# Subtracting attention thresholds on GpSimd for eight pairs of heads, in place of a second score pass for two of them

## The chip, the cores and the metric

The kernel runs on one core of a Trainium2 chip. The metric is device time in microseconds for one execution; lower is better. The core has engines that each work through their own list of instructions in order and wait for one another by semaphores: TensorE (PE, matmuls), VectorE (DVE), ScalarE (ACT), GpSimd (POOL), and SyncE (SP), which here only issues transfers.

## The reference

Attention with a threshold, for 8 batches of 8 heads with 576 positions and 64 channels, followed by a feed-forward block on the 4608 tokens.

```python
scores = scale * np.matmul(q, k.transpose(0, 1, 3, 2))
thresh = np.max(scores, axis=-1, keepdims=True) - tau
scores = np.where(scores >= thresh, scores, -1000000000.0)
scores = scores - np.max(scores, axis=-1, keepdims=True)
attn = np.exp(scores)
attn = attn / (np.sum(attn, axis=-1, keepdims=True) + 1e-09)
attn_out = np.matmul(attn, v)
# (B,H,S,D) -> (B*S, H*D) is x, 4608 x 512
h = x @ w_in                                   # 512 x 2048
g = h * (1.0 / (1.0 + np.exp(-1.702 * h)))
out = g @ w_out                                # 2048 x 512
```

q, k and v are float32; the two weight matrices arrive as float64 and are turned into float32 on the chip.

## The kernel before

**Pairs.** Two heads of a batch make a pair, so there are 32 pairs, four to a batch, numbered from 0 here as in the code. Scores are kept transposed: keys on partitions, queries along the free dimension. A pair has nine steps of 64 keys per head (two heads and two halves of the queries fill 128 partitions and 576 columns). Two steps make a tile of 128x1152, so a pair has four such tiles, 0 to 3, and tile 4, which has one step and 576 columns.

**What is done for a pair `n`.** `load_qk` and `load_v` issue the transfers (SP). `prep` transposes q and k (DVE, L498). `scores` computes a step on PE (L514), `keep` copies it from PSUM to SBUF (ACT, L531), `in_groups` takes maxima of a tile (DVE, L537), `over_tiles` and `over_halves` finish the maximum and take the gap off it. The threshold of each query must then stand on all partitions that hold its column. There are three ways to that:

- `spread_max`: one transpose on DVE (L618).
- by DMA (pairs in BY_DMA): `turn_rows` on DVE, `row_out` to DRAM (L627) and `row_in` back with the row repeated (L636), both issued by SP.
- by a second score pass (pairs in TWICE): `row_blocks` on DVE (L585, L587) places the thresholds for a matmul; `again` computes each step of scores a second time on PE and adds minus the threshold by a second group of matmuls (L604); `mask_one` reads that from PSUM on ACT (L612), one step at a time.

In the first two ways `sub` (L642) subtracts the thresholds from a tile in SBUF, and `mask` (L648) makes everything below zero hugely negative. In all three, `exps` (L652) takes exponentials of a tile on ACT. `values` multiplies by v on PE (L663) and `sums_by_pe` by ones (L663, into `den`); in later pairs the sums are `in_groups` with add on DVE, and `turn_sums`, `sums_out` and `sums_in` send their reciprocals through DRAM. `place_x` (DVE, L765) divides and writes the result into x, transposed.

**Feed-forward.** x is cut into 18 blocks of 256 tokens. The first two (`first_blocks`) go through `mm1_0` (L820), `tanh`, `gelu_0` (L826) and `mm2` (L802); the first needs all four pairs of batch 0. Later blocks use `mm1` (L780) and seven products (`product`, L971) in place of eight, whose sums of halves are made by POOL (`s_sums`, L937 to L939, and `s_last`); the last four blocks use seven products for the first matmul too (`product1`, L885; `w_sum` L859, `x_sum` L868).

**Weights.** There are 32 pieces, 16 of w_in and then 16 of w_out. For each, POOL issues two DMAs (`load_w`, L449 and L450), DVE takes the exponent (L460), masks and combines the mantissa (L474, L478), ACT turns the exponent to a power of two (L468), and DVE multiplies (`cv_end`, L486). Pieces pass through a few slots; a load waits until its slot has been freed by an earlier `cv_end`. The first six loads are held back behind q and k of pairs 2 and 3 by `hold`.

**Order.** Nothing is scheduled by hand and nothing by the framework: each step is a `task` with an engine, a cost in microseconds, a rank and its predecessors, and `run_in_order` plays them in a list schedule while the program is being built. Whenever an engine is free in that play, it takes the ready task of lowest rank whose buffers are free, and the instructions are emitted in that order. A step's rank is the pair's number plus a bias from one of four tables: EARLY for pairs 0 to 3, SECOND for 4 to 7, LATER for the rest, CV for the weights. W_RANK gives the base ranks of the weight pieces. Transfers are tasks of two servers of their own, DMS for those that SP issues and DMW for the weights. The order that results is fixed in the program; on the chip each engine follows it, whatever the real durations are.

The ways in which pairs differ are set by a few constants:

```python
JOINT = 7
TWICE = (2, 3)
BY_POOL = {}
SUMS_BY_PE = (0, 1, 2, 3, 4)
BY_DMA = (0, 1, *range(4, NP))
SUMS_BY_DMA = range(5, NP)
SHARED = 0.2 if BY_POOL else 0.0
```

JOINT is the first pair whose scores are interleaved on PE with the values of the pair two before it. BY_POOL maps a pair to the tiles whose `sub` runs on POOL; it is empty, so every `sub` runs on DVE. SHARED is added to the planner's cost of two weight steps on DVE.

Of the kernel before, what the change touches and what calls it, by code (L numbers as in the profile page):

```python
# [30 lines left out]
def kernel(  # L31
# [97 lines left out]
    for x in ("raw0", "raw1", "qkT0", "qkT1", "mb"):  # L129
# [3 lines left out]


    EARLY = {
        "again": -7.56,
        "exps": -11.91,
        "in_groups": 11.71,
        "keep": 5.71,
        "load_qk": 5.18,  # L140
        "load_v": 30.97,
        "mask": 4.9,
        "mask_one": 3.1,
        "one_group": -15.86,
        "one_row": 7.15,
        "over_halves": -2.83,
        "over_tiles": 6.14,
        "place_x": -3.25,
        "prep": 2.3,
        "row_blocks": 1.94,  # L150
        "row_in": 22.91,
        "row_out": -2.33,
        "scores_run": 18.47,
        "spread_max": -1.73,
        "spread_sums": 1.81,
        "sub": 11.02,
        "sums_by_pe": -0.88,
        "sums_in": -30.06,
        "sums_out": 1.15,
        "turn_rows": 7.89,  # L160
        "turn_sums": 3.77,
        "values": 12.67,
        "w_sum": -3.43,
        "x_sum": -40.7,
    }
    SECOND = {
        "again": 1.9,
        "exps": -5.59,
        "in_groups": 24.66,
        "keep": 31.08,  # L170
        "load_qk": 4.38,
        "load_v": 10.96,
        "mask": 1.77,
        "mask_one": -3.71,
        "one_group": 2.55,
        "one_row": -9.14,
        "over_halves": -14.0,
        "over_tiles": 20.14,
        "place_x": -19.87,
        "prep": 13.95,  # L180
        "row_blocks": -7.77,
        "row_in": -19.84,
        "row_out": -10.94,
        "scores_run": -8.9,
        "spread_max": -3.11,
        "spread_sums": 11.27,
        "sub": 23.58,
        "sums_by_pe": 28.33,
        "sums_in": 6.64,
        "sums_out": 8.13,  # L190
        "turn_rows": -23.75,
        "turn_sums": -20.53,
        "values": -5.6,
        "w_sum": 2.52,
        "x_sum": -6.03,
    }
    LATER = {
        "again": 0.33,
        "exps": -3.93,
        "in_groups": 13.94,  # L200
        "keep": -8.05,
        "load_qk": -10.23,
        "load_v": -5.75,
        "mask": 20.67,
        "mask_one": 13.2,
        "one_group": 4.78,
        "one_row": -18.27,
        "over_halves": -1.32,
        "over_tiles": -0.36,
        "place_x": 19.41,  # L210
        "prep": -1.19,
        "row_blocks": -5.02,
        "row_in": 1.23,
        "row_out": 9.63,
        "scores_run": -23.96,
        "spread_max": -9.44,
        "spread_sums": 7.45,
        "sub": 5.73,
        "sums_by_pe": -10.99,
        "sums_in": -0.62,  # L220
        "sums_out": -1.68,
        "turn_rows": 3.05,
        "turn_sums": 5.98,
        "values": -17.83,
        "w_sum": -2.8,
        "x_sum": 11.74,
    }
    CV = {
        "cv_end": -4.16,
        "cv_ex": -2.85,  # L230
        "cv_frac": -20.95,
        "cv_power": -9.52,
        "load_w": -10.23,
    }

    LAG = {"PE": 0.26, "DVE": 0.18, "ACT": 0.22, "POOL": 0.18, "SP": 0.1}
# [4 lines left out]
    def task(engine, cost, rank, f, *a, after=(), take=(), give=(), lag=None):  # L241
        if lag is None:
            lag = LAG[engine]
        if 0 <= rank < LAST:
            biases = EARLY if a[0] < NPAIR else SECOND if a[0] < 2 * NPAIR else LATER
            rank += CV[f.__name__] if f.__name__ in CV else biases.get(f.__name__, 0.0)
        tasks.append((engine, cost, rank, f, a, [x for x in after if x is not None],
                      take, give, lag))
        return len(tasks) - 1
# [71 lines left out]

    rebias = const.tile([P, 1], FP32, name="rebias")
    JOINT = 7
    TWICE = (2, 3)
    BY_POOL = {}

# [45 lines left out]
    def own(n, *pools):  # L374
        return tuple(x + "_apart" for x in pools) if n in APART else pools
# [134 lines left out]
    def scores(n, j):  # L510
        ps = psA.tile([P, 2, 512], FP32, name="ps", tag="ps")
        for h in range(2):
            for c in range(2):
# [4 lines left out]
                )  # L518
        if j == NK - 1 and n not in TWICE:
            del mats[n, 0], mats[n, 1]  # L520
# [32 lines left out]
    def over_halves(n):  # L553
        r = stats[n, ALU.max]
        o = work.tile([P, QB], FP32, name="fold", tag="fold", bufs=1)
        for x in (1, 3) if n in BY_DMA else range(4):
            nc.vector.tensor_scalar(
                out=o[ts(x ^ 1, 32)], in0=r[ts(x, 32)], scalar1=gap[ts(x, 32)], scalar2=None,
                op0=ALU.subtract,
            )  # L560
        if n in TWICE:
            for x, y in ((0, 0), (1, 2), (2, 1), (3, 3)):
# [4 lines left out]
            return  # L567
        if n in BY_DMA:
            for x in (0, 2):
# [69 lines left out]
    def sub(n, t):  # L639
        s = sT[n, t].rearrange("p u h s -> p u (h s)")  # L640
        engine = nc.gpsimd if t in BY_POOL.get(n, ()) else nc.vector
        engine.tensor_tensor(  # L642
# [361 lines left out]
    NP = B * NPAIR  # L1004
# [38 lines left out]


    SUMS_BY_PE = (0, 1, 2, 3, 4)
    BY_DMA = (0, 1, *range(4, NP))
    SUMS_BY_DMA = range(5, NP)
    LEAD = 6
    WHOLE = 6

    SHARED = 0.2 if BY_POOL else 0.0
    FFU = 1.727
    T_RANK = FIRST

    W_RANK = (8.59, 39.29, 35.34, 31.13, 0.54, 8.21)
    ready_w, w_loads, w64 = [], [], 0
    for i in range(len(pieces)):
        y = 0 if i < NDC else 2 if i < n_in else 4
        n = NDC if i < NDC else n_in - NDC if i < n_in else n_in
        first = (0, 0, NDC, 0, n_in)[y]  # L1060
        rank = W_RANK[y] + (W_RANK[y + 1] - W_RANK[y]) * (i - first) / n
        if not wide:
# [205 lines left out]
    for n in range(NP):  # L1268
# [64 lines left out]
        else:  # L1333
            for js in [range(x, x + 3) for x in range(0, NK, 3)] if n >= WHOLE else [[x] for x in range(NK)]:
# [3 lines left out]
                    take=("psA",) * len(js) + new,  # L1338
                    give=own(n, "qkT0", "qkT1") if js[-1] == NK - 1 and n not in TWICE else (),
                )  # L1340
# [3 lines left out]
        a = task("DVE", 0.35, r, over_tiles, n, ALU.max, after=mx)  # L1344
        quick = n in BY_DMA or n in TWICE
        a = task(
            "DVE", 1.05 if not quick else 1.3 if n in TWICE else 0.8, r, over_halves, n,
            after=[a, tau_done], take=("row",) if quick else (),
        )
        if n in TWICE:  # L1350
            m = task("DVE", 0.6, r, row_blocks, n, after=[a], take=own(n, "mb"), give=("row",))
        elif n in BY_DMA:
            a = task("DVE", 0.21, r, turn_rows, n, after=[a])
# [7 lines left out]
        for t in range(NKT + 1):  # L1361
            tail = t == NKT
            if n in TWICE:
# [7 lines left out]
                continue  # L1371
            pool = t in BY_POOL.get(n, ())
            a = task(
                "POOL" if pool else "DVE", (1.45 if pool else 0.67) if tail else 2.7 if pool else 1.35,
                r, sub, n, t, after=[y for y, x in subs if tail or x in (None, pool)],
# [89 lines left out]
```

## Time and profile before

| | |
|---|---|
| times of three runs | 1336.89, 1333.9, 1336.76 us; median 1336.76 |
| the profiled execution | 1336.89 us, span 1335.1 us |
| PE busy | 1278.8 us, 96% |
| DVE busy | 990.5 us, 74% |
| ACT busy | 647.7 us, 49% |
| POOL busy | 248.1 us, 19% |
| chain that ended last | PE 67%, DVE 12%, DMA 8%, ACT 7% |
| L514, scores | 2304 matmuls, 172.4 us |
| L604, the second score pass | 288 matmuls, 24.1 us |
| L642, `sub` on DVE | 149 instructions, mean 1306 ns |
| L652, `exps` on ACT | 160 instructions, mean 1249 ns |

Busy time is how long an engine had an instruction in work; the difference of span and PE's busy time, 56.3 us, is what TensorE stood idle. Consecutive matmuls overlap, so that their own durations add up to more than the busy time. The shares are means over a start, in which loading, conversion of weights and the first pairs are all under way, and a long steady part. In rows of the timeline the first two numbers are the start from the beginning of the span and the length in microseconds, and brackets at the end tell how long the engine stood idle before it and what it waited for.

### The profile page before, as it was taken

The numbers are of one execution on the slowest core, as the hardware profiler recorded it, in microseconds if no ns is written. First come the engines' busy times: TensorE is split into PE (matmuls) and PEld (weight loads), VectorE is DVE, ScalarE is ACT, GpSimd is POOL, SyncE is SP. The second block draws the span as 40 slices with busy tenths as digits, with TensorE's granted clock in tenths as the row PEclk, the third lists the DMA queues.
The fourth block names the chain that finished last, engine by engine and source line by source line (L and its number), as shares of the span: only waits on it lengthen the run. The fifth ranks groups of instructions, "written<-read, shape, count | busy, mean of one in ns | idle before, by whom it ended". The sixth has DMA issues, their size and how long they took to land.

```text
span 1335.1 us, 23381 instructions
## 1 busy us (share of the span) xinstructions
PE 1278.8 (96%) x9416; PEld 988.3 (74%) x9416; DVE 990.5 (74%) x1600; ACT 647.7 (49%) x838; POOL 248.1 (19%) x301
## 2 busy tenths in 40 slices
PE   5599799899999999999999999999999999999998
PEld 2456585457777777778878777777777878888887
DVE  6798799888887788778877777778877863652642
ACT  4786465767454555555455445455555540210210
POOL 1121111003112120212130201112121216120120
PEclk8799899999999999999999999999999999999999
DMA  8579686547232222222323232222222120000000
GB/s 152 212 161 271 226 250 124 106 91 124 63 70 55 57 44 59 55 53 55 70 54 70 46 79 55 62 47 50 55 55 53 37 61 2 16 1 24 8 1 32
DMA packets 259634, 103.53 MB, mean 78 GB/s; under 512 B 233926, under 2 KB 244934, under 8 KB 259526
## 3 DMA queue, kind: packets, MB, share of 16 engines
q1 hardware_dynamic: 245798, 64.00, 22.8%
q0 software_dynamic: 11360, 37.74, 9.4%
q8 instruction: 74, 1.21, 0.4%
q10 hardware_dynamic: 2368, 0.30, 0.2%
q14 instruction: 34, 0.28, 0.1%
HBM read 88.10 MB, written 9.70 MB: 73 GB/s over the span
## 4 chain that ended last, share of the span: by engine, by line
PE 67%; DVE 12%; DMA 8%; ACT 7%; SPq 3%; issue 2%; DVEq 0%; POOL 0%; ACTq 0%
PE ops L971 22%; PE hps L780 16%; PE pv L663 8%; PE ps L514 8%; PE ps L885 4%; PE ps L971 4%; DVE part L537 3%; ACT arena L652 3%; PE ops L885 3%; DMA arena<-row 3%; DVE arena L642 3%; ACT arena L648 2%; DMA arena<-in_k_dram 2%; DMA arena<-in_q_dram 1%; PE hps L820 1%
## 5 line engine op out<-in xcount | busy, mean ns | idle before, releaser
L537 DVE TRANSPOSE_TENSOR_REDUCE part<-arena 128x36 f32<-128x1152 f32 (+1 forms) x295 | 359.6, 1239 | 63.6 <-ACT arena L531 54.0
L780 PE MATMUL hps<-xT,w_in 128*128 128x256 f32 x1536 | 339.8, 381 | 5.9 <-DVE arena L792 5.6
L780 PEld LDWEIGHTS hps<-xT,w_in 128*128 128x128 f32 x1536 | 289.8, 190 | 54.8 <-DVE arena L792 10.7
L648 ACT ACTIVATE arena<-arena 128x1152 f32<-128x1152 f32 (+1 forms) x150 | 158.5, 1057 | 164.7 <-DVE arena L642 164.7
L531 ACT COPY arena<-ps 128x576 f32<-128x576 f32 x288 | 170.3, 645 | 140.4 <-PE ps L514 140.4
L642 DVE TENSOR_TENSOR arena<-arena 128x1152 f32<-128x1152 f32 (+1 forms) x149 | 188.4, 1306 | 37.7 <-DMA arena<-row 37.7
L971 PE MATMUL ops<-w_out,arena 128*128 128x256 f32 x896 | 203.3, 381 | 1.6 <-DVE arena L792 1.3
L652 ACT ACTIVATE arena<-arena,shift,scl 128x1152 f32<-128x1152 f32 (+1 forms) x160 | 199.9, 1249 | 4.1
L514 PE MATMUL ps<-arena 64*64 64x288 f32 x2304 | 172.4, 416 | 23.1 <-DVE neg L1030 8.3
L971 PEld LDWEIGHTS ops<-w_out,arena 128*128 128x128 f32 x896 | 168.9, 190 | 30.3 <-DVE arena L792 4.2
L937 POOL TENSOR_TENSOR arena<-arena 128x256 f32<-128x256 f32 x56 | 49.1, 877 | 651.6 <-DVE arena L792 540.6
L663 PE MATMUL pv<-arena 64*64 64x288 f32 x2176 | 160.0, 409 | 0.0
L971 PE MATMUL ops<-arena 128*128 128x256 f32 x672 | 150.6, 380 | 0.0
L514 PEld LDWEIGHTS ps<-arena 64*64 64x64 f32 x2304 | 84.8, 136 | 86.7 <-ACT arena L531 24.6
L971 PEld LDWEIGHTS ops<-arena 128*128 128x128 f32 x672 | 127.2, 190 | 19.3 <-issue 2.2
L789 ACT ACTIVATE th<-hps 128x512 f32<-128x512 f32 x112 | 65.9, 589 | 142.8 <-PE hps L780 127.9
L663 PEld LDWEIGHTS pv<-arena 64*64 64x64 f32 x2176 | 81.7, 134 | 55.0 <-issue 11.2
L993 DVE SCALAR_TENSOR_TENSOR osb<-ops,osb 128x256 f32<-128x256 f32 x98 | 39.3, 413 | 81.2 <-PE ops L971 79.4
L792 DVE SCALAR_TENSOR_TENSOR arena<-th,hps 128x512 f32<-128x512 f32 x96 | 63.9, 665 | 38.6 <-ACT th L789 36.9
L820 PE MATMUL hps<-xT,w_in 128*128 128x256 f32 x256 | 59.1, 392 | 7.0 <-DVE arena L826 7.0
L820 PEld LDWEIGHTS hps<-xT,w_in 128*128 128x128 f32 x256 | 49.7, 196 | 16.6 <-DVE arena L826 7.9
L498 DVE STREAM_TRANSPOSE arena<-arena 128x576 f32<-128x576 f32 x64 | 45.8, 744 | 20.5 <-DMA arena<-in_q_dram 15.5
(123 smaller groups left out, 1084.5 us busy)
## 6 DMA issues: line engine op xcount, KB each, us to landing
arena<-in_v_dram SPq DMA_DIRECT2D x128, 144.0 KB
arena<-in_q_dram SPq DMA_DIRECT2D x128, 72.0 KB
out_dram<-osb SPq DMA_DIRECT2D x36, 256.0 KB
arena<-in_k_dram SPq DMA_DIRECT2D x124, 72.0 KB
arena<-row SPq DMA_DIRECT2D x60, 144.0 KB
arena<-row_s SPq DMA_DIRECT2D x54, 144.0 KB
w_out<-in_moe_w_in_dram POOLq DMA_DIRECT2D x12, 512.0 KB, 7.6
arena<-in_moe_w_out_dram POOLq DMA_DIRECT2D x12, 512.0 KB, 3.9
```

The costliest lines, as they stand in the source:

```text
L514: nc.tensor.matmul(ps[ts(c, KT), h, 0:SH], lhsT=mats[n, 1][ts(h, D), ts(j, KT)], rhs=mats[n, 0][ts(h, D), ts(c, SH)], start=True, stop=True,)
L531: nc.scalar.copy(out=sT[n, t][:, u], in_=pss.pop((n, j))[:, :, 0:SH])
L537: nc.vector.tensor_reduce(out=stats[n, op][:, t * 2 * QB : min(2 * t + 2, NK) * QB], in_=sT[n, t].rearrange("p u h (g d) -> p (u h g) d", ...
L642: engine.tensor_tensor(out=s, in0=s, in1=mbs[n].unsqueeze(1).to_broadcast(list(s.shape)), op=ALU.subtract)
L648: nc.scalar.activation(out=s, in_=s, func=AF.Prelu, alpha=STEEP)
L652: nc.scalar.activation(out=s, in_=s, func=AF.Exp, scale=scl, bias=shift)
L663: nc.tensor.matmul(o[c][ts(h, D), 0:SH], lhsT=left(j, h)[ts(c, KT)], rhs=sT[n, t][ts(c, KT), u, h, :], start=(j == 0), stop=(j == NK - 1),)
L780: nc.tensor.matmul(hidden[j][:, ts(f, BLK)], lhsT=w_in[:, c, ds((f * HF + j) * P, P)], rhs=xTs[blk][:, c, :], start=(c == 0), stop=(c == N ...
L789: nc.scalar.activation(out=ths[j], in_=hidden[j], func=AF.Tanh, scale=GELU_SCALE / 2)
L820: nc.tensor.matmul(hidden[j][:, ts(i, BLK)], lhsT=w_in[:, c, ts(j, P)], rhs=xTs[i][:, c, :], start=(c == 0), stop=(c == NDC - 1),)
L885: nc.tensor.matmul(places[j, x], lhsT=left[:, c, ts(j, P)], rhs=right[:, c, :], start=(c == 0), stop=(c == 1),)
L971: nc.tensor.matmul(banks[blk][k][:, ts(o, HM)], lhsT=left[:, j, :], rhs=right[:, j, :], start=(j == 0), stop=(j == HF - 1),)
```

## The change

Pairs 2 and 3 no longer compute their scores twice: TWICE is empty, and `again`, `mask_one` and `row_blocks` are no longer called. Pair 3 joins BY_DMA, so its thresholds go through DRAM; pair 2 is in neither set, so `spread_max` is used for it. BY_POOL now names tiles 1, 3 and 4 for each of pairs 0 to 7, so their `sub` runs on POOL, with planner costs of 2.7 us (1.45 us for tile 4); tiles 0 and 2 stay on DVE. SHARED becomes 0.2. All the biases in the four rank tables and the six numbers of W_RANK are replaced, which gives another order on every engine. The functions themselves are the same.

```diff
     EARLY = {
-        "again": -7.56,
-        "exps": -11.91,
...
+        "exps": -4.82,
...
     CV = {
-        "cv_end": -4.16,
-        "cv_ex": -2.85,
-        "cv_frac": -20.95,
-        "cv_power": -9.52,
-        "load_w": -10.23,
+        "cv_end": -15.81,
+        "cv_ex": -1.62,
+        "cv_frac": -18.99,
+        "cv_power": -9.27,
+        "load_w": -20.76,
     }
...
     JOINT = 7
-    TWICE = (2, 3)
-    BY_POOL = {}
+    TWICE = ()
+    BY_POOL = dict.fromkeys(range(8), (1, 3, 4))
...
     SUMS_BY_PE = (0, 1, 2, 3, 4)
-    BY_DMA = (0, 1, *range(4, NP))
+    BY_DMA = (0, 1, *range(3, NP))
...
-    W_RANK = (8.59, 39.29, 35.34, 31.13, 0.54, 8.21)
+    W_RANK = (22.52, 3.88, 13.03, 23.19, 4.19, 0.55)
```

The step that the change moves, and its place in the plan:

```python
def sub(n, t):
    s = sT[n, t].rearrange("p u h s -> p u (h s)")
    engine = nc.gpsimd if t in BY_POOL.get(n, ()) else nc.vector
    engine.tensor_tensor(
        out=s, in0=s, in1=mbs[n].unsqueeze(1).to_broadcast(list(s.shape)), op=ALU.subtract
    )
...
    pool = t in BY_POOL.get(n, ())
    a = task(
        "POOL" if pool else "DVE", (1.45 if pool else 0.67) if tail else 2.7 if pool else 1.35,
        r, sub, n, t, after=[y for y, x in subs if tail or x in (None, pool)],
        give=own(n, "mb") if tail else (),
    )
```

More of the change, by code (lines that the diff above doesn't have):

```diff
@@ L135 @@
     EARLY = {
-        "again": -7.56,
-        "exps": -11.91,
[L138 to L143, printed above, removed]
-        "one_group": -15.86,
[L145 to L164, printed above, removed]
+        "exps": -4.82,
+        "in_groups": 13.97,
+        "keep": -8.17,
+        "load_qk": 16.71,
+        "load_v": 10.24,
+        "mask": 6.69,
+        "one_group": -15.86,
+        "one_row": 16.12,
+        "over_halves": -19.01,
@@ L165 @@
+        "over_tiles": -3.6,
+        "place_x": -53.15,
+        "prep": -7.58,
+        "row_in": 34.46,
+        "row_out": 20.86,
+        "scores_run": 15.16,
+        "spread_max": 14.44,
+        "spread_sums": 1.31,
+        "sub": 6.54,
+        "sums_by_pe": 25.13,
+        "sums_in": 1.84,
+        "sums_out": 32.63,
+        "turn_rows": -14.29,
+        "turn_sums": -9.74,
+        "values": 31.66,
+        "w_sum": -11.75,
+        "x_sum": -17.48,
     }
     SECOND = {
-        "again": 1.9,
@@ L168 @@
[L168 to L174, printed above, removed]
-        "one_group": 2.55,
[L176 to L195, printed above, removed]
+        "exps": 9.8,
+        "in_groups": 15.75,
+        "keep": 5.63,
+        "load_qk": 2.6,
+        "load_v": -7.97,
+        "mask": 6.41,
+        "one_group": 2.55,
+        "one_row": -21.83,
+        "over_halves": 5.0,
+        "over_tiles": -7.55,
@@ L196 @@
+        "place_x": -7.21,
+        "prep": -1.01,
+        "row_in": -3.96,
+        "row_out": -17.44,
+        "scores_run": -0.9,
+        "spread_max": -8.71,
+        "spread_sums": 10.47,
+        "sub": 11.98,
+        "sums_by_pe": 44.98,
+        "sums_in": 12.4,
+        "sums_out": 26.07,
+        "turn_rows": -22.24,
+        "turn_sums": 10.99,
+        "values": 9.61,
+        "w_sum": 9.41,
+        "x_sum": -13.68,
     }
     LATER = {
-        "again": 0.33,
-        "exps": -3.93,
@@ L200 @@
[L200 to L205, printed above, removed]
-        "one_group": 4.78,
[L207 to L226, printed above, removed]
+        "exps": 19.95,
+        "in_groups": 15.85,
+        "keep": 0.95,
+        "load_qk": -35.26,
+        "load_v": -4.44,
+        "mask": 12.76,
+        "one_group": 4.78,
+        "one_row": -26.62,
+        "over_halves": 5.32,
+        "over_tiles": -23.66,
+        "place_x": -24.36,
@@ L227 @@
+        "prep": -6.1,
+        "row_in": -0.68,
+        "row_out": -15.78,
+        "scores_run": -5.98,
+        "spread_max": -2.3,
+        "spread_sums": 12.68,
+        "sub": -8.42,
+        "sums_by_pe": -20.72,
+        "sums_in": -14.05,
+        "sums_out": -11.28,
+        "turn_rows": -0.52,
+        "turn_sums": -0.51,
+        "values": -18.44,
+        "w_sum": 3.97,
+        "x_sum": -11.26,
     }
     CV = {
-        "cv_end": -4.16,
-        "cv_ex": -2.85,
-        "cv_frac": -20.95,
```

## The prediction

> **What bounds the kernel now.** I read the page's slices of the span first, then busy time by stretch, then the timeline of each engine up to 330 us.
>
> ```profile
> PE   5599799899999999999999999999999999999998
> DVE  6798799888887788778877777778877863652642
> DMA  8579686547232222222323232222222120000000
> ```
> Each digit covers 33 us. TensorE has gaps only in the first 400 us; the change lies in the first eight pairs, so inside the first ten slices.
>
> ```profile
> 60.00:124.00 64.00, 61.02 (x936) 38.39 (x928) 58.24 (x127) 50.40 (x73) 10.05 (x18) 0.97 0.74 190
> 77.00:109.00 32.00, 31.30 (x504) 18.33 (x500) 29.03 (x52) 29.96 (x42) 7.91 (x14) 1.00 0.81 210
> 124.00:212.00 88.00, 80.97 (x496) 61.61 (x494) 76.04 (x126) 50.96 (x67) 17.34 (x32) 0.96 0.74 223
> 300.00:1335.00 1035.00, 1021.88 (x6972) 829.29 (x6962) 734.93 (x1164) 451.65 (x584) 205.34 (x213) 1.00 0.22 49
> ```
> After the length come the busy us of PE, its weight loads, DVE, ACT and POOL. From 300 us on TensorE is busy 1021.9 of 1035: there the time is a fixed amount of matmul work, and the change can only move the moment at which it begins. Between 77 and 109 us, where pairs 2 and 3 are masked, PE (31.3 of 32), ACT (30.0) and DVE (29.0) are all full.
>
> **Part 1: the second score pass goes.** TWICE is emptied, so 18 calls of `again` leave TensorE.
>
> ```profile
> 79.30 0.67 PE L604 MATMUL ps<-arena 64*64 64x288 f32 x8
> 79.78 0.67 PE L604 MATMUL ps<-arena,minus 64*64 64x288 f32 x8
> ...
> 114.20 3.09 PE L663 MATMUL pv<-arena,arena 64*64 64x288 f32 x48
> ```
> Groups of eight start 0.485 apart, one call is two groups, 0.97 us: 18 x 0.97 = 17.5 us of PE work. It is not 17.5 us of time, because ACT runs without a gap over the same stretch:
>
> ```profile
> 89.32 1.17 ACT L612 ACTIVATE arena<-ps 128x576 f32<-128x576 f32 x2
> ...
> 94.33 4.40 ACT L531 COPY arena<-ps 128x576 f32<-128x576 f32 x8
> ...
> 107.39 0.87 ACT L652 ACTIVATE arena<-arena,shift,scl 128x576 f32<-128x576 f32 x1
> 120.20 0.94 DVE L765 TENSOR_TENSOR xT<-pv,arena 128x256 f32<-128x256 f32 x4
> ```
> The masks of both pairs take ACT 18 x 0.61 = 11.0 us now and 8 x 1.15 + 2 x 0.67 = 10.5 after; the last exponential of pair 3 ends at 108.3 either way. What PE's relief does buy is after that: the value products of pairs 2 and 3 (144 matmuls, 0.0605 us each, 8.7 us) are all left until 107.9 to 119.2, and pair 3 is placed at 120.2. With PE free they can follow the exponentials. 108.3, the last tile's products (1.0) and the way from the sums to the placing (2.3, as pair 1 from 69.3 to 71.6) give 111.6, with some queueing 113: **-7 us** for the start of the feed-forward (bounds 0 and -17.5).
>
> **Part 2: pair 2 and pair 3 get thresholds another way.** DVE loses `row_blocks` and the eight small steps for each (0.97 + 0.96 + 0.21 + 0.46 = 2.6). Pair 2 gets `over_halves` in five steps (1.15), `spread_max` (0.78, as L748) and two subtractions (2 x 1.36): 4.65, so +2.0. Pair 3 gets 0.49 + 0.49 + 0.21 + 2.72 = 3.9, +1.3, and its thresholds travel through DRAM: two `row_out` and two `row_in` DMAs on SP's queue. That trip is in the trace:
>
> ```profile
> 38.06 0.63 SPq L627 DMA_DIRECT2D row<-flat  x2
> 51.58 5.16 DVE L642 TENSOR_TENSOR arena<-arena 128x1152 f32<-128x1152 f32 x4 [6.42 <-DMA arena<-row]
> 53.47 19.98 SPq L398 DMA_DIRECT2D arena<-in_v_dram  x8
> ```
> Pair 1's row turned at 38.0, its first subtraction started at 51.6 and DVE sat idle 6.4 us for it: 13.5 us. Pair 5 (178.5 to 186.4) took 7.9, pair 7 (229.9 to 243.4) 13.5. I take 13.5: DMA is as busy at 77 to 109 (0.81) as in the first 60 us (0.82), and the third line shows SP stuck 20 us issuing eight transfers of v, behind which a row would stand. Pair 3's row would be turned at 84.0 (82.76 + 1.2), 2.0 later for pair 2's added DVE steps and 3.5 later for part 3's blocking, so 89.5; with 13.5 and one subtraction (1.36) ACT gets its first tile at 104.3. ACT now begins pair 3 at 89.3. Of these 15.0 us, the eight copies and three weight steps that ACT does between 92.3 and 98.7 cover 6.4. Queued behind the waiting mask are the copies of the next pairs, which wait for PSUM, then PE. **+8.6 us**; bounds 0 (7.9 us, no blocking: 93.3, lateness under the cover) and +28.6 (SP's 20 us in front).
>
> **Part 3: POOL subtracts tiles 1, 3 and 4 of pairs 0 to 7.** No such operation of this size is in the trace. POOL alone takes 0.73 us for 256 columns (L937) and 1.27 for 512 (L859); the line through both gives 2.62 for 1152 and 1.41 for 576, 6.65 a pair, 53 us in all, where DVE loses 2 x 1.36 + 0.75 = 3.5 a pair. Inside a pair this is covered: ACT needs 1.15 + 1.35 for a tile, so tile 4 is wanted 10 us after tile 0, and even in strict turns the five subtractions end after 9.4. The cost is what DVE and POOL do to each other:
>
> ```profile
> 311.12 0.73 POOL L937 TENSOR_TENSOR arena<-arena 128x256 f32<-128x256 f32 x1 [2.06 <-DVE arena L792]
> 311.77 3.12 DVE L642 TENSOR_TENSOR arena<-arena 128x1152 f32<-128x1152 f32 x2
> 311.94 1.74 POOL L938 TENSOR_TENSOR arena<-arena 128x256 f32<-128x256 f32 x1
> ...
> 1106.95 0.69 DVE L868 TENSOR_TENSOR arena<-xT 128x512 f32<-128x512 f32 x1
> ...
> 1109.12 1.22 DVE L868 TENSOR_TENSOR xT<-xT 128x512 f32<-128x512 f32 x1
> ```
> Beside DVE's subtraction the POOL step goes from 0.73 to 1.74, and two DVE tiles from 2.63 to 3.12: 0.49 lost for two POOL steps worth 1.46, 34%. In the second place DVE loses 0.53 for one of 0.73, 73%. So 6.65 us of POOL cost DVE 2.3 to 4.8 a pair; I take the middle, 3.5, which cancels the 3.5 saved. The stage where DVE's load sets the pace is 124 to 212 (76 of 88 us, with 8.6 idle at one late q load); pairs 4 and 5 fall in it: **0 us**, bounds -7.0 (no blocking) and +2.6. In pairs 6 and 7 PE covers either sign.
>
> The Trainium skill, "SBUF — State Buffer", section "Who interferes with whom", speaks against this part: a DVE instruction with two SBUF inputs and a GpSimd one that reads SBUF exclude each other for the whole instruction, the later one fully blocked. The rows here show mutual loss, but 34 to 73% of it on DVE; by the full rule pairs 4 and 5 would lose 13.3 - 7.0 = 6.3 us there and the sum below would be 1348 (an estimate from that page).
>
> **Part 4: POOL's queue.** POOL also issues the weight loads, each as soon as DVE has freed a slot.
>
> ```profile
> 202.54 0.53 POOL L449 DMA_DIRECT2D arena<-in_moe_w_out_dram  x1 [4.35 <-ACT arena L648]
> 203.33 12.18 PE L802 MATMUL ops<-w_out,arena 128*128 128x512 f32 x28
> 211.35 0.69 DVE L486 SCALAR_TENSOR_TENSOR w_out<-arena 128x512 f32<-128x512 int32 x1
> ```
> The last piece is converted at 212.0; `mm2` begins at 203.3 and needs it seven steps of 1.73 later, at 215.4: 3.4 us of slack. Pair 5's subtractions (186 to 200) now stand between these loads: 6.65 - 3.4 = **+3.3 us** (bounds 0, and +11.2 if a POOL step also waits 7.9 for its row). Pair 4's fall into POOL's idle 129.4 to 146.4.
>
> **Part 5: new ranks and W_RANK** redraw the order of everything. load_w moves from -10.2 to -20.8, so loads stand earlier; I cost the whole at 0, bounds -8.6 (DVE's longest idle, for the q load at 131.6 to 140.2, goes) and +8.6 (another one comes).
>
> **Sum.** -7 + 8.6 + 0 + 3.3 = +4.9 against the profiled 1336.89 (span 1335.1 and 1.8 around it; the median shown is 1336.76): 1341.8, so **1342**.
>
> **Rivals.** *Freed engines are freed time (faster).* Parts 1 and 3 count (-7 and -7), pair 3's row takes 7.9 and stays under ACT's cover, loads come early enough: 1336.9 - 14 = 1323. For it: the three full engines at 77 to 109, the one full DVE stage. Against: 13.5 us seen twice for the row. *No change.* The row takes 7.9 but blocking holds: 89.5 + 9.3 - 89.3 - 6.4 = +3.1; -7 + 3.1 + 3.3: 1336.3. *POOL's queue is the new bound (much slower).* A subtraction that waits for its row holds every weight load behind it; at pairs 0 and 1, where the first w_in loads are issued (27 to 41), one such wait is 13.5: 1342 + 13.5 = 1355. It decides once the row lands later than the load's slot is free; POOL's waits then name the row. *The change is mostly the ranks*, and parts 1 to 4 vanish in a reshuffle: either sign, within the bounds of part 5.
>
> **How the numbers follow.** This kernel's runs tell 0.3% (4 us) from no change. Forecast 0.38 (own range 1341 to 1350), POOL's queue 0.17: slower 0.55. No change 0.17. Faster 0.28. The range 1323 to 1360 leaves out about half of the faster case's spread below and the end of the queue case above.
>
> **What would show it.** PE busy down by some 17 us with the idle time before 300 us up by more; no L604; ACT idle for pair 3's row, 8 us or so; POOL L642 at 2.6 us alone and longer beside DVE's; weight loads behind it. I am wrong if pair 3 is placed well before 120 us, or if the second block's `mm1` starts earlier than now.

## The result: slower by 1.2%, and the profile after

The changed kernel takes 1352.17 us (median of 4 runs, 1350.22 to 1353.76) beside 1336.83 us before (1333.9 to 1337.4): ratio 1.0119, 95% interval 1.0097 to 1.0140. That is 15.3 us more; the prediction said 1342, 5 us more, and 1360 as the upper end. The profiled execution has a span of 1348.4 us. The helpers' lines are nine lower than before: `sub` is L633, `scores` L505, the weight steps L451 to L477.

The slices of the span of the changed kernel, each digit the busy share of 33.7 us in tenths:

```profile
PE   5467898979999999999999999999999999999998
DVE  6987978898988888777777787878787874562642
```

The table by stretches of the changed kernel (start and end; length; then busy us of PE, weight loads, DVE, ACT and POOL; then the granted clock, the DMA share and GB/s):

```profile
60.00:124.00 64.00, 38.21 (x488) 26.20 (x484) 55.93 (x85) 46.03 (x55) 29.82 (x26) 0.79 0.74 193
77.00:109.00 32.00, 20.40 (x284) 11.84 (x287) 25.61 (x34) 23.15 (x31) 18.55 (x18) 0.84 0.81 248
124.00:212.00 88.00, 77.38 (x598) 60.17 (x591) 71.80 (x117) 39.93 (x56) 26.62 (x30) 0.95 0.58 171
300.00:1335.00 1035.00, 1032.17 (x7144) 833.72 (x7137) 759.55 (x1198) 464.07 (x610) 206.79 (x214) 1.00 0.23 51
```

TensorE has 1267.5 us of work in place of 1278.8, and yet the span is longer: the work that left became idle time, and more with it. Between 60 and 124 us PE is busy 38.2 us (61.0 before), and its granted clock there is 0.79 (0.97 before). POOL is busy 29.8 us in that stretch (10.1 before). From 300 us on PE is nearly full in both kernels (1032.2 of 1035 us, 1021.9 before), so the loss is made in the first 300 us. The feed-forward starts at 134.8 us (123.9 before), `mm2` at 221.1 (203.3), the third block's `mm1` at 313.5 (291.2 for its first eight matmuls, 301.9 for the rest).

Where DVE's time went is to be seen in the timeline. First the changed kernel around pair 0's and pair 4's subtractions (start, busy us, engine, line, operation, out<-in; x2 stands for two instructions in one row):

```profile
37.24 5.75 DVE L548 TENSOR_SCALAR fold<-red,gap 32x18 f32<-32x18 f32 x2
37.49 5.19 POOL L633 TENSOR_TENSOR arena<-arena 128x1152 f32<-128x1152 f32 x2
...
151.22 9.36 DVE L633 TENSOR_TENSOR arena<-arena 128x1152 f32<-128x1152 f32 x2
152.80 6.56 POOL L633 TENSOR_TENSOR arena<-arena 128x1152 f32<-128x1152 f32 x3
```

The two steps at 37.24 belong to pair 1. The same steps in the timeline of after_dve2, the same plan with those subtractions on DVE (a run below):

```profile
38.72 0.49 DVE L548 TENSOR_SCALAR fold<-red,gap 32x18 f32<-32x18 f32 x2
```

Two steps on 32x18 elements, 0.49 us when alone, take 5.75 us: they end 0.3 us after POOL has finished two subtractions. At 151.2 two DVE subtractions (2.6 us alone) take 9.36, and end 1.2 us after POOL has finished three. POOL itself keeps its pace at these two places, 5.19 for two; elsewhere it is held as well (6.88 for two at 53.7), and its 16 full tiles have a mean of 3.3 us. The profile counts the standing still as DVE's busy time, so no wait is printed: only the same step in a run without POOL's subtractions shows it.

### The profile page after: what moved, and what is told of

The parts are those of the page before. It is cut to its first block, busy times and chain, and to the rows that moved or that the text cites. A ratio compares the mean times of both kernels' runs of the same rounds, so it can differ in the third digit from the quotient of the medians.

```text
span 1348.4 us, 22852 instructions
## 1 busy us (share of the span) xinstructions
PE 1267.5 (94%) x9128; PEld 984.7 (73%) x9128; DVE 1014.9 (75%) x1577; ACT 638.1 (47%) x830; POOL 312.5 (23%) x325
## 4 chain that ended last, share of the span: by engine, by line
PE 73%; DVE 12%; DMA 6%; ACT 5%; issue 3%; POOL 1%; SPq 1%; DVEq 0%; POOLq 0%; ACTq 0%
PE ops L962 23%; PE hps L771 22%; PE pv L654 8%; PE ps L505 7%; PE ps L876 4%; PE ps L962 4%; DMA arena<-row 3%; PE ops L876 3%; DVE part L528 3%; DVE arena L633 3%; DMA row<-flat 2%; ACT arena L522 1%; ACT arena L643 1%; ACT arena L639 1%; PE hps L811 1%
## 5 line engine op out<-in xcount | busy, mean ns | idle before, releaser
L528 DVE TRANSPOSE_TENSOR_REDUCE part<-arena 128x36 f32<-128x1152 f32 (+1 forms) x295 | 357.2, 1235 | 51.4 <-ACT arena L522 31.9
L639 ACT ACTIVATE arena<-arena 128x1152 f32<-128x1152 f32 (+1 forms) x160 | 165.8, 1060 | 160.9 <-DVE arena L633 141.2
L505 PE MATMUL ps<-arena 64*64 64x288 f32 x2304 | 177.5, 421 | 39.8 <-DVE arena L489 16.3
L633 DVE TENSOR_TENSOR arena<-arena 128x1152 f32<-128x1152 f32 (+1 forms) x136 | 194.2, 1470 | 26.2 <-DMA arena<-row 25.9
L643 ACT ACTIVATE arena<-arena,shift,scl 128x1152 f32<-128x1152 f32 (+1 forms) x160 | 194.9, 1249 | 1.4
L505 PEld LDWEIGHTS ps<-arena 64*64 64x64 f32 x2304 | 87.1, 137 | 104.2 <-ACT arena L522 38.6
L633 POOL TENSOR_TENSOR arena<-arena 128x1152 f32<-128x1152 f32 (+1 forms) x22 | 60.9, 2808 | 47.2 <-DMA arena<-row 33.8
```

The costliest lines, as they stand in the source:

```text
L505: nc.tensor.matmul(ps[ts(c, KT), h, 0:SH], lhsT=mats[n, 1][ts(h, D), ts(j, KT)], rhs=mats[n, 0][ts(h, D), ts(c, SH)], start=True, stop=True,)
L528: nc.vector.tensor_reduce(out=stats[n, op][:, t * 2 * QB : min(2 * t + 2, NK) * QB], in_=sT[n, t].rearrange("p u h (g d) -> p (u h g) d", ...
L633: engine.tensor_tensor(out=s, in0=s, in1=mbs[n].unsqueeze(1).to_broadcast(list(s.shape)), op=ALU.subtract)
L639: nc.scalar.activation(out=s, in_=s, func=AF.Prelu, alpha=STEEP)
L643: nc.scalar.activation(out=s, in_=s, func=AF.Exp, scale=scl, bias=shift)
```

## The experiments

Three theories for the loss: POOL's subtractions hold DVE up (1); the new ranks made a bad order (2); pair 3's trip through DRAM in place of the second score pass (3). The first two kernels tried keep the order of the kernel that they start from, since only the instruction's engine is changed inside `sub`, and not the planner's task.

**b_same**: the kernel before, with 18 subtractions moved (pairs 2 and 3 have no `sub` in it).

```diff
-        engine = nc.gpsimd if t in BY_POOL.get(n, ()) else nc.vector
+        engine = nc.gpsimd if n < 8 and t in (1, 3, 4) else nc.vector
```

> The kernel before with its own order on every engine; only the engine of 18 subtractions changes: tiles 1, 3 and 4 of pairs 0, 1, 4, 5, 6 and 7 go to POOL at the place that they had in the plan. Theory 1 (POOL's subtractions hold DVE up for their whole length, so DVE loses more than the 3.5 us a pair that it is spared): slower, 1341 to 1348. Theory 2 (the loss comes from the new ranks, that is from the order): no change, 1334 to 1339. Theory 3 (the loss comes from pair 3's trip through DRAM in place of the second score pass): no change either.

1344.31 us, ratio 1.0053 (1.0033 to 1.0073): slower by 7.8 us against 1336.51 for the kernel before beside it. That is in theory 1's range; theories 2 and 3 alone have nothing to explain it with. DVE was busy 998.6 us in place of 990.5 although 20.7 us of subtractions (12 x 1.35 + 6 x 0.75) had left it: 28.8 us of standing still, 8.1 net.

**after_dve** and **after_dve2** (the same kernel twice): the changed kernel, with the 24 subtractions moved back.

```diff
-        engine = nc.gpsimd if t in BY_POOL.get(n, ()) else nc.vector
+        engine = nc.vector
```

> The changed kernel with its own order on every engine; only the engine of the 24 POOL subtractions changes: all run on DVE, at the place that they had in the plan. Theory 1: most of the 15 us come back, 1338 to 1344, and no short DVE instruction takes several us. Theory 2 and theory 3: 1349 to 1355, since order and trip are kept; a little slower still if the 3.5 us a pair that DVE takes back count.

> The same kernel as after_dve, for a narrower interval and beside the two others: 1333, ratio 0.996 to 0.9995, if its gain over the kernel before is real; 1.000 if not.

1333.41 us, ratio 0.9977 (0.9957 to 0.9997), and in the second, with more runs, 1331.87, ratio 0.9962 (0.9946 to 0.9979). Theory 1 expected 1338 to 1344, and more than that came back. So in this order POOL's subtractions cost 18.8 to 20.3 us, more than the whole loss, and the rest of the change gains 3 to 5 us. This version is faster than both kernels. Its two profiled executions took 1339.3 and 1329.1 us, so single profiles of it are not compared by their ends.

**c_ranks** and **ac**: what the planner makes of the parts. c_ranks is the kernel before with the new tables (`again`, `mask_one` and `row_blocks` keep their old ranks); ac is the changed kernel with nothing on POOL.

```diff
# ac, against the changed kernel
-    BY_POOL = dict.fromkeys(range(8), (1, 3, 4))
+    BY_POOL = {}
```

> The kernel before (second score pass for pairs 2 and 3, all subtractions on DVE) with the new ranks and W_RANK; the ranks of again, mask_one and row_blocks stay. Theory 2: slower by most of the 15 us, 1346 to 1354. Theories 1 and 3: 1333 to 1341.

> No second score pass (pair 2 by the transpose, pair 3 through DRAM), new ranks, but no subtraction on POOL, and the planner knows it. Theory 3: 1347 to 1354, as the trip and the lost cover stay. Theory 1: 1337 to 1343. Theory 2: not told apart from theory 3 by this run alone, but by the one with new ranks only.

c_ranks: 1338.15 us, ratio 1.0016 (0.9995 to 1.0036), so the ranks by themselves cost next to nothing on the old set of tasks. ac: 1345.16, ratio 1.0054 (1.0035 to 1.0072), between what theory 1 (1337 to 1343) and theory 3 (1347 to 1354) expected. By its parts it is after_dve, with every subtraction on DVE and the same ranks, and it is 12 us slower: the two differ in the order alone, and in SHARED, which only the planner reads. So the ranks did well with the planner's tasks of the changed kernel and badly with another set. The old ranks without the second pass were not tried.

**What in POOL's work does it.** Three mechanisms were open: the reading blocks DVE (1a), ACT waits for a slow result (1b), weight loads stand in POOL's list behind subtractions that wait for their rows (1c). dve_read and dve_fill leave all subtractions on DVE and put other work, estimated to be of about the same length, into POOL's list.

```diff
# dve_read: reads two tiles
+        if t in BY_POOL.get(n, ()):
+            for w in (324, 324, 324) if t < NKT else (324, 164):
+                nc.gpsimd.tensor_tensor(
+                    out=dummy[:, 0:w], in0=dummy[:, 0:w], in1=mbs[n][:, 0:w], op=ALU.subtract
+                )
# dve_fill: writes only, but for one column
+        if t in BY_POOL.get(n, ()):
+            nc.gpsimd.tensor_copy(out=stop, in_=mbs[n][:, 0:1])
+            for _ in range(7 if t < NKT else 3):
+                nc.gpsimd.memset(dummy, 0.0)
```

> As after_dve (1333.4: every subtraction on DVE, order of the changed kernel), but where a subtraction stood in POOL's list, POOL now subtracts columns of mb from a spare tile of its own that nobody reads: three steps of 324 columns (two of 324 and 164 for tile 4), by the line through 0.73 at 256 and 1.27 at 512 as long as the subtraction was (2.62 and 1.41). They wait for the thresholds as it did. Nobody waits for their result, and the output is right. Theory 1a (POOL reading SBUF holds DVE up): 1343 to 1354, short DVE steps of 2 us and more beside them. Theory 1b (POOL's subtraction is slow, and ACT waits for its result): 1331 to 1337. Theory 1c (weight loads wait in POOL's list behind subtractions that wait for their row): 1343 to 1354 too, but then also in dve_fill.

> As dve_read, but POOL's filler only writes: a copy of one column of mb (which waits for the thresholds) and seven memsets of 324 columns (three for tile 4), estimated at 0.36 us each from 0.15 for 64 and 0.20 for 128 columns. Same wait and about the same time in POOL's list, no reading beside the one column. Theory 1a: 1331 to 1337. Theory 1c: 1340 or more. Theory 1b: 1331 to 1337.

dve_read: 1360.54 us, ratio 1.0154 (1.0110 to 1.0199), 27 us above after_dve and above the 1354 that theory 1a allowed. dve_fill: 1336.10, ratio 0.9988 (0.9966 to 1.0011), 2.7 to 4.2 above after_dve and after_dve2; the intervals overlap, so this small difference is not firm. In the traces POOL was at its filler for 82.0 us in dve_read and 72.9 in dve_fill, and for 65.4 at the subtractions in the changed kernel, so the lengths are alike but not equal. Nobody waits for the filler's result, so 1b cannot make the 27; the wait in POOL's list is about the same in both, so 1c is worth about what dve_fill shows at most. The timeline of dve_read at pair 0 (`sub` on DVE is L634 there, the filler L639):

```profile
37.22 6.64 POOL L639 TENSOR_TENSOR dummy<-dummy,arena 128x324 f32<-128x324 f32 x6
37.01 2.31 DVE L634 TENSOR_TENSOR arena<-arena 128x1152 f32<-128x1152 f32 x1
41.08 1.86 DVE L562 SCALAR_TENSOR_TENSOR flat<-red,gap,fold 32x18 f32<-32x18 f32 x2
```

The timeline of dve_fill at the same place:

```profile
38.45 2.91 POOL L640 MEMSET dummy<- 128x324 f32 x7
38.50 0.76 DVE L549 TENSOR_SCALAR fold<-red,gap 32x18 f32<-32x18 f32 x2
```

Beside POOL's reading, one DVE subtraction takes 2.31 in place of 1.35 and two small steps 1.86 in place of 0.49; beside seven memsets the small steps take 0.76. DVE's busy time is 1033.7 us in dve_read and 1002.1 in after_dve2: 31.6 us of holding, and 27 to 29 us of time.

So 1a is shown to be able to make the loss. It is not shown that 1b adds nothing in the changed kernel, where ACT does wait for POOL: 19.6 us in seven waits for POOL's subtractions and 19.7 for DVE's, beside 23.8 for DVE's alone in after_dve2. One of the longest, in the timeline of the changed kernel:

```profile
96.20 1.41 POOL L633 TENSOR_TENSOR arena<-arena 128x576 f32<-128x576 f32 x1
97.64 0.69 ACT L639 ACTIVATE arena<-arena 128x576 f32<-128x576 f32 x1 [5.92 <-POOL arena L633]
```

This is pair 2's tile 4. POOL had finished tiles 1 and 3 at 83.9, but the loads of six weight pieces stand before tile 4 in its list, some of which waited for earlier transfers. In b_same ACT waits only 4.1 us in all for POOL's results, so there the holding has little beside it; in the changed kernel no run tells the two apart.

**after_early** and **after_late**: POOL subtracts for pairs 0 to 3 only, or for 4 to 7 only, in the changed kernel's order.

```diff
# after_late: n >= 4
+        engine = nc.gpsimd if n < 4 and t in BY_POOL.get(n, ()) else nc.vector
```

> The changed kernel with its order, where only pairs 0 to 3 keep their subtractions on POOL; those of pairs 4 to 7 run on DVE. If the loss is made while the first four pairs and w_in go on (DVE 48 of 60 us busy): 1343 to 1350. If it is made in pairs 4 to 7, where DVE sets the pace of gelu: 1334 to 1339.

> The other half: POOL for pairs 4 to 7, DVE for pairs 0 to 3. Early theory: 1334 to 1341; late theory: 1345 to 1351. If both halves count, the two runs lie above 1333.4 by amounts that add up to some 19 us.

1340.10 us (ratio 1.0012, 0.9988 to 1.0036) and 1343.76 (1.0045, 1.0021 to 1.0070): 6.7 and 10.4 above 1333.41, together 17.0 of the 18.8. Each lies between the ranges of the early and the late theory: both halves count, and neither theory of one place holds.

**Pair 3's trip, dve_spread3.** As after_dve; pair 3 is spread by DVE's transpose.

```diff
     def turn_rows(n):
+        if n == 3:
+            spread_max(n)
+            return
...
     def row_out(n):
+        if n == 3:
+            return
```

> As after_dve, but pair 3's thresholds are spread by DVE's transpose at the place of turn_rows (as pair 2's are) and do not go through DRAM; DVE does 1.3 us more, SP issues four transfers less. If pair 3's trip sets the start of the feed-forward (prediction: 8.6 us): 1324 to 1329. If the trip is covered or something else is as late: 1331 to 1336.

1333.81 us, ratio 0.9979 (0.9965 to 0.9994): no gain over after_dve, so in that order the trip costs nothing. The trip was real in the changed kernel, as the timeline of the changed kernel shows (brackets: the idle time before, and what ended it):

```profile
91.36 0.70 SPq L618 DMA_DIRECT2D row<-flat  x2
97.22 1.39 SPq L627 DMA_DIRECT2D arena<-row  x2
106.17 1.36 DVE L633 TENSOR_TENSOR arena<-arena 128x1152 f32<-128x1152 f32 x1 [3.62 <-DMA arena<-row]
```

When it goes, something else is as late, in the timeline of dve_spread3:

```profile
97.10 15.34 SPq L378 DMA_DIRECT2D arena<-in_k_dram  x4
119.40 0.78 DVE L489 STREAM_TRANSPOSE arena<-arena 128x576 f32<-128x576 f32 x1 [4.79 <-DMA arena<-in_k_dram]
120.32 2.20 PE L505 MATMUL ps<-arena 64*64 64x288 f32 x16 [7.68 <-DVE arena L489]
```

Without the row, pair 3's subtractions end at 106.5, but the next pair's k is still being issued, 15.3 us for four transfers; DVE stands for it until 119.4, when it can transpose that k, and PE has been idle for 7.7 us when it gets the result at 120.3.

**The worth of PE's relief, dve_triple and dve_extra.** Both put matmul work into after_dve that changes nothing in the result.

```diff
# dve_triple, in scores
-        for h in range(2):
+        for h in [y for _ in range(3 if n in (2, 3) else 1) for y in range(2)]:
# dve_extra, in by_values
+                        w = BANK if n in (2, 3) and h == 0 else SH
+                        rhs = sT[n, t].rearrange("p u h s -> p u (h s)")
                         nc.tensor.matmul(
-                            o[c][ts(h, D), 0:SH], lhsT=left(j, h)[ts(c, KT)],
-                            rhs=sT[n, t][ts(c, KT), u, h, :],
+                            o[c][ts(h, D), 0:w], lhsT=left(j, h)[ts(c, KT)],
+                            rhs=rhs[ts(c, KT), u, ds(h * SH, w)],
```

> As after_dve, but each score matmul of pairs 2 and 3 is issued three times into the same place (the result is the same): 18 steps of 0.97 us, 17.5 us of PE work, put back about as much as the second score pass took, without its way through ACT. If PE's relief was worth the 7 us that the prediction gave it: 1340 or more. If PE has that time to spare in the first 135 us: 1331 to 1336.

> As after_dve (1333.4 and 1331.9), but the matmuls of values and sums of pairs 2 and 3 for the first head of the pair run over 512 columns in place of 288; the columns beyond are read by nobody, and the output is right. That is 36 steps longer by 39% (both heads in turn) to 78% (heads side by side), 6.8 to 13.6 us of PE work by the 0.485 us of a step, and it stands where the second score pass stood, after the thresholds, between the tiles that ACT hands over. If PE's relief there was worth about its length: 1338 to 1346. If ACT sets the pace there and PE has time to spare: 1331 to 1335.

dve_triple: 1350.71 us, ratio 1.0100 (1.0080 to 1.0119). It does not answer the question, because the work stands in another place: before the maxima, on which thresholds, exponentials and everything behind them wait. Pair 2's scores in the timeline of after_dve2:

```profile
26.51 6.89 PE L505 MATMUL ps<-arena 64*64 64x288 f32 x64 [6.41 <-DVE arena L489]
```

And in that of dve_triple:

```profile
26.64 14.63 PE L505 MATMUL ps<-arena 64*64 64x288 f32 x192 [6.41 <-DVE arena L489]
```

They end at 41.3 in place of 33.4, 7.9 us later. Pair 3's, which stand between matmuls of values, end at 93.2 in place of 79.7, 13.5 us later, of which 7.9 can be the first delay carried on. PE is not full there, but it is the head of a chain. dve_extra has the work after the thresholds, where the second pass stood: 1335.98 us, ratio 0.9999 (0.9984 to 1.0014), between the two ranges that were expected and 2.6 to 4.1 above after_dve and after_dve2, for some 10 us of matmul work (nine steps of pair 2's values take 6.87 us in place of 4.36, and there are four such groups). The interval is apart from after_dve2's and overlaps after_dve's, so about a third of the work's length is the best reading, and not a firm one.

## Why the prediction was right in sign and short in size

The forecast (slower, 1342) had the sign, and 1352 lies in the range of 1323 to 1360, though above the forecast's own 1341 to 1350. The sign was in part luck. The sum holds +5.1 us for pair 3's trip, for which dve_spread3 found 0; without them it is -7 + 3.5 + 0 + 3.3 = -0.2, no change. What made the loss, DVE and POOL in each other's way, was named and charged with 3.5 us: two errors of opposite sign, of which the second is the larger.

**Part 3 is the term that failed, by its size.** The step was "6.65 us of POOL cost DVE 2.3 to 4.8 a pair; I take the middle, 3.5, which cancels the 3.5 saved". POOL's price for a step alone was right: 2.6 us a tile (5.19 for two) and 1.41 for tile 4; being held as well, its 24 subtractions took 65.4 us in place of 53. DVE's loss was not the middle. Its busy time is 1014.9 us; after_dve2 has 1002.1 with 24 subtractions more, 16 x 1.35 + 8 x 0.75 = 27.6, so 1014.9 - 1002.1 + 27.6 = 40.4 us were spent standing, 5.0 a pair, above the upper bound of 4.8.

The lower bound came from a miscount. The "34%" sets DVE's 0.49 us against two POOL steps. L938 ended at 313.68, between DVE's two tiles. The next POOL step in the timeline of the kernel before is this one:

```profile
313.63 1.84 POOL L939 TENSOR_TENSOR arena<-arena 128x256 f32<-128x256 f32 x1
```

It ended at 315.47, 0.58 us after DVE's second tile (314.89), so nearly all of its own 0.73 came after DVE. Only one step of 0.73 stood between the tiles: 0.49 us is 67% of it, close to the 73% of the second place. By 67 to 73%, DVE would lose 4.5 to 4.9 us a pair (an estimate from these rows), near the 5.0 measured. Groups of the first 300 us show how it is spread (count, busy us, mean ns of one, idle time before), first in the changed kernel:

```profile
L633 DVE TENSOR_TENSOR arena<-arena 128x1152 f32<-128x1152 f32 x16 | 40.2, 2537 | 10.9 <-DMA arena<-row 10.9
L548 DVE TENSOR_SCALAR fold<-red,gap 32x18 f32<-32x18 f32 x20 | 9.8, 492 | 0.6
L477 DVE SCALAR_TENSOR_TENSOR w_in<-w_out 128x512 f32<-128x512 int32 x12 | 14.3, 1192 | 5.8 <-ACT w_out L459 5.7
```

The same groups in after_dve2:

```profile
L633 DVE TENSOR_TENSOR arena<-arena 128x1152 f32<-128x1152 f32 x36 | 47.1, 1350 | 17.6 <-DMA arena<-row 17.5
L548 DVE TENSOR_SCALAR fold<-red,gap 32x18 f32<-32x18 f32 x22 | 5.0, 229 | 0.7
L477 DVE SCALAR_TENSOR_TENSOR w_in<-w_out 128x512 f32<-128x512 int32 x12 | 8.2, 686 | 0.6 <-ACT w_out L459 0.4
```

The loss in time is larger than DVE's net 12.8 us. A likely reason, not tested by itself, is what is held: the two steps at 37.2 come before the turning of pair 1's row, which starts at 43.5 in place of 39.8. Charged to part 3 were 3.5 us (in pair 3's lateness); 18.8 to 20.3, less dve_fill's 2.7 to 4.2, were measured: about 16, with ACT's waits for POOL's results in it.

Whether "In pairs 6 and 7 PE covers either sign" held is not shown. PE stands 7.2 us for a copy by ACT at 284.5, just after pair 7's held subtractions, but at the same place also 3.9 us in after_dve2 and 7.6 in dve_fill.

The Trainium skill, "SBUF — State Buffer", section "Who interferes with whom", was set against the rows and not followed. Its rule, that the later one is fully blocked, fits the subtractions at 151.2 (9.36 us for two of 1.35). The sum by it was 1348; the measured 1352 lies beyond. The rule was applied to pairs 4 and 5 only, and that sum too holds the 5.1 us of the trip.

**Part 4** is not contradicted: +3.3 predicted for loads behind POOL's subtractions, 2.7 to 4.2 with the writing filler, which is within the noise and has some held DVE steps in it (DVE busy 1005.8 us beside 1002.1). The other way round, a subtraction behind loads (pair 2's tile 4), was not thought of.

**Part 1** held as far as it was tried: -7 for 17.5 us of PE work, 0.4 us for each; dve_extra found 0.26 to 0.41 per us in that place. PE's busy time fell by 11.3 us only: the 2304 score matmuls, as many as before, were busy 177.5 us in place of 172.4. ACT's stretch was not quite without a gap (1.15 us at 99.9).

**Part 2** had the trip right (13.5 us predicted, turned at 91.3 and used at 106.2: 14.9) and its worth wrong: +5.1 us without the blocking, 0 in dve_spread3. In the changed kernel ACT stood 2.7 us before pair 3's first mask at 107.6, not the 8 or so that was to show it. The working named ACT's other work as the only cover; the next pair's k, 15 us in the issuing on SP's queue, ends as late. That SP's queue can be full was read in the trace before (20 us for v) and drawn on only for the upper bound.

**Part 5** was costed at 0 within 8.6. Parts 1, 2 and 5 together gave -3 to -5 us where -7 + 5.1 + 0 = -1.9 stood, and ac against after_dve shows that an order can be worth 12 us, beyond the bound.

The rival of freed engines (1323) fell with the blocking: its gain is there, but a third of it. The rival of POOL's queue gave nearly the right number (1355) for a wrong reason: dve_fill has POOL's wait for the rows in front of the weight loads, and not the loss.

## What to carry to other kernels

An elementwise step moved from DVE to GpSimd is not free for DVE where DVE's own steps beside it are of the kinds that were held here (`tensor_tensor`, `scalar_tensor_tensor`, `tensor_scalar` in SBUF): DVE lost 40.4 us for 27.6 saved. Set most of GpSimd's time (here 40.4 of 53 us) against what DVE is spared. To learn what a moved step costs, change the engine of the emitted instruction and keep the plan; a new plan for the same work moved this kernel by 12 us. And before a wait is priced, look for the next thing that lands as late.

## What the runs showed of the hardware that was not expected

- A DVE step can be held through several GpSimd instructions and not just one: 5.75 us for two steps of 0.49, beside two subtractions of 2.6.
- `tensor_scalar` steps, with one tensor as input, are held too: L451 on 128x512 has a mean of 586 ns in the changed kernel's first 300 us and 427 in after_dve2 (the group in w_out's slots). With a filler that mainly writes, those steps still lose (L466 in dve_fill 524 ns against 424), while steps with two inputs lose nothing (subtractions 1349 against 1350 ns). The Trainium skill, "SBUF — State Buffer", section "Who interferes with whom", has both halves of this.
- Not every DVE step is held: the maxima (L528 on 128x1152) have a mean of 1348 ns in the changed kernel's first 300 us and in after_dve2, the transposes (L489) 754 and 760.
- TensorE's granted clock is low in a stretch in which it idles much: 0.79 between 60 and 124 us, where it was busy 38 of 64, and 0.97 in the kernel before, where it was busy 61. What this costs by itself was not tried.
